# Pooled attention and a gated MLP on one core: the order in which batch 0 of the attention is loaded, cast and normalised

## The chip, the core and the metric

The kernel runs on one core of a Trainium2 chip. A core has a matrix engine (TensorE; PE in the profile, its weight loads PEld), three engines for elementwise work (VectorE: DVE, ScalarE: ACT, GpSimd: POOL), and a queue engine, SyncE (SP), that issues DMAs. PE writes its results into PSUM, from where DVE and ACT read them; all else works on SBUF. Each engine runs its own instructions in program order and waits on semaphores for the others. DMAs are issued from SP's queue or from GpSimd's queue; only the latter convert fp32 to bf16 under way here.

The metric is device time in microseconds (us), the median of several executions. The profile comes from one further execution.

## What is computed

Cut from the reference, with B = 8 batches, H = 8 heads, S = 576 tokens and D = 64:

```python
k_p = k.reshape(B, H, 72, 8, D).mean(axis=3)      # keys and values pooled over 8 tokens
v_p = v.reshape(B, H, 72, 8, D).mean(axis=3)
scores = (1 / sqrt(D)) * q @ k_p.transpose(0, 1, 3, 2)
attn = softmax(scores)                            # over the 72 pooled keys
x = (attn @ v_p).transpose(0, 2, 1, 3).reshape(B * S, H * D)   # 4608 x 512
h = x @ w_in                                      # 512 -> 2048
out = (h * cos(h)) @ w_out                        # 2048 -> 512
```

Inputs and output are fp32; the matmuls take bf16.

## The kernel before

**Tiling.** The 4608 tokens go through the MLP in nine chunks of 512 (`NT`). For each chunk the up projection computes 16 blocks of 128 features in eight pairs (`fp`): `up_mm` makes the 4 matmuls (k chunks 0 to 3 of the 512 inputs) for each block of a pair into one of three two-bank PSUM tiles (`banks[fp % 3]`), `up_g` takes the cosine on ACT (Sin with a bias of pi/2, L363) and multiplies on DVE into `g_sb` (L366), which frees the PSUM tile. The down projection (`down_mm`, L369) follows with 64 matmuls, and `down_out` copies and stores. Attention of batch b+1 is placed between the down matmuls of chunk b, at hand-written positions (`fill`). Engine orders are the program order: the kernel runs under a manual schedule, in which only the semaphores are put in automatically.

**The opening.** Batch 0 has nothing to hide behind. Its work is a chain written out by hand after `warm_up` (L452 on), and the change touches this and the loads ahead of it:

- *Loads.* The first half of k (heads 0 to 3) comes in fp32 over SP's queue into a part of `g_sb` (L401) and is cast by ACT in one piece (L402). GpSimd's queue brings, converted, q's first half, k's second half, q's second half and v (`load_even`, L84), then builds `identity`, then issues the weights (`load_w_in`, L112) and the loads of batch 1.
- *Pooling.* `groups` is a 0/1 matrix made by DVE (L420 to L424). `pool_k_mm` (L159) pools two head pairs by 36 matmuls with the keys as the stationary operand, into 64 rows by 72 columns for each pair. `put_kk` (L132) copies them four times (two halves of rows twice) into `kk`. `pool_v_mm` (L167) pools v; one DVE copy (L169) puts it into `vz`, which a memset had filled with 8.0 (L425).
- *Queries.* `q_transpose_mm` (L202) transposes 18 blocks of 128 columns of q on PE; DVE or ACT copies them into `qT` (L203).
- *Units.* A unit is 256 tokens of four heads: `us[0]` and `us[1]` are the two token ranges of heads 0 to 3, `us[2]` and `us[3]` those of heads 4 to 7 (the last 64 tokens, `REST`, come later). `scores` makes 8 matmuls (L221) and an Exp on ACT (L228) per pair of banks. `sums_first` multiplies the Exp's result by `ones` on PE (L276) and forms the inverse of the sums on ACT as Ln (L280) and Exp (L281). `values_then` makes the values' matmuls (L318) and multiplies by the inverse on DVE into `xT` (L320). `sums_two` and `values_two` (L284 to L309) do both for two units together, over two banks, with one Ln, one Exp and one multiplication of 1024 columns; batch 1 uses them.
- *Warm-ups.* `warm_up(n, bank)` makes n matmuls on constants whose result is not used.
- *Hand-over.* `up_mm(0, 0, 0, 2)` and `up_mm(0, 1, 0, 2)` (L356) start the first two pairs of chunk 0 with k chunks 0 and 1, which need heads 0 to 3 alone; the loop finishes them with k chunks 2 and 3. `exp_tables` and `sin_tables` switch ACT's function table.

Of the kernel before, what the change touches and what calls it, by code (L numbers as in the profile page):

```python
# [9 lines left out]
FP32 = mybir.dt.float32  # L10
BF16 = mybir.dt.bfloat16
# [3 lines left out]
POOL = 8  # L15
# [4 lines left out]
def kernel(  # L20
# [9 lines left out]
    nc = tc.nc  # L30
    B, H, S, D = q.shape
    Sp = S // POOL
# [4 lines left out]
    KCH = d_model // 128  # L37
    FFCH = d_ff // 128
    NT = n_tokens // TILE
    ROW = S // 64  # L40
# [84 lines left out]
    def v_part(b):  # L125
        return vz[b % 2][:, :, 0:4:3, :]
# [25 lines left out]
    def pool_k_mm(b, bank, pj0, pj1):  # L152

        kb = staged["k", b]
        ps = bank[:, 0:(pj1 - pj0) * Sp].rearrange("p (j n) -> p j n", n=Sp)
        for pj in range(pj0, pj1):
            for t in range(ROW):
                for rows in half:
                    nc.tensor.matmul(ps[rows, pj - pj0, :], lhsT=kb[rows, pj, t, :], rhs=groups[rows, t, :],  # L159
                                     start=(t == 0), stop=(t == ROW - 1))  # L160
        return lambda copy: put_kk(b, ps, pj0, pj1, copy)

    def pool_v_mm(b, pair):
        vb = staged["v", b]
        for t in range(ROW):
            for hp, rows in enumerate(half):
                nc.tensor.matmul(pair[:Sp, hp, 0:KCH * D], lhsT=groups[rows, t, :], rhs=vb[rows, :, t, :],  # L167
                                 start=(t == 0), stop=(t == ROW - 1))
        nc.vector.tensor_copy(out=v_part(b).rearrange("p j a d -> p a j d"),  # L169
                              in_=pair[:Sp, :, 0:KCH * D].rearrange("p a (j d) -> p a j d", j=KCH))  # L170
# [25 lines left out]
    def q_transpose_mm(b, bank, g0, g1):  # L196

        if ("qT", b) not in att:
            qT_tile(b)
        ps = bank.bitcast(BF16)[:, 0:(g1 - g0) * 128].rearrange("p (g n) -> p g n", n=128)  # L200
        for g in range(g0, g1):
            nc.tensor.matmul(ps[:, g - g0, :], q_flat(b)[:, g * 128:(g + 1) * 128], identity, is_transpose=True)  # L202
        return lambda copy: copy(out=att["qT", b][:, g0:g1, :], in_=ps)  # L203
# [6 lines left out]
    def scores(b, u, pair):  # L210
        scores_mm(b, u, pair)
        scores_exp(b, u, pair)
# [57 lines left out]
    def sums_first(b, u, cs):  # L270

        (c0, n), (h0, nh) = u
        ex = att["ex", b, u]
        for i in range(nh):
            hp = i % 2
            nc.tensor.matmul(cs[hp * 64:hp * 64 + 64, (i // 2) * n:(i // 2 + 1) * n], lhsT=ones[:Sp, :],  # L276
                             rhs=ex[:, ex_col(u, i):ex_col(u, i) + n])
        w = nh * n // 2
        lnc, inv = inverse_tile(w)
        nc.scalar.activation(out=lnc, in_=cs[:, 0:w], func=ACTF.Ln)  # L280
        nc.scalar.activation(out=inv, in_=lnc, func=ACTF.Exp, scale=-1.0)  # L281
        att["inv", b, u] = inv
# [63 lines left out]
    def sin_tables():  # L346
        nc.scalar.preload_act_table_set("trig_and_small")  # L347
# [49 lines left out]

    kv_even_tiles(0)
    q_tile(0)
    k_first = g_sb.rearrange("p f n -> p (f n)").bitcast(FP32)[:, 0:2 * ROW * D]  # L400
    nc.sync.dma_start(out=k_first.rearrange("p (j n) -> p j n", j=2), in_=even_view(k, 0, 0, 2))  # L401
    nc.scalar.copy(out=staged["k", 0][:, 0:2].rearrange("p j t d -> p (j t d)"), in_=k_first)  # L402

    row_of = consts.tile([128, ROW], FP32, name="row_of")
    for rows in half:
# [2 lines left out]
    first_of = consts.tile([128, Sp], FP32, name="first_of")  # L408
    nc.gpsimd.iota(first_of, pattern=[[POOL, Sp]], base=0, channel_multiplier=0,
                   allow_small_or_imprecise_dtypes=True)  # L410
    load_even(staged["q", 0], 0, q, 0, 2)
    load_even(staged["k", 0], 0, k, 2, 4)
    load_even(staged["q", 0], 0, q, 2, 4)
    load_even(staged["v", 0], 0, v)
    identity = consts.tile([128, 128], BF16, name="identity")
    make_identity(nc, identity)
    dist, sign = (w.rearrange("p f m -> p (f m)").bitcast(FP32)[:, 0:ROW * Sp].rearrange("p (t n) -> p t n", n=Sp)
                  for w in w_out_sb[2:4])
    groups = consts.tile([128, ROW, Sp], BF16, name="groups")
# [2 lines left out]
    nc.vector.scalar_tensor_tensor(out=sign, in0=dist, scalar=1.0 - POOL, in1=dist, op0=ADD,  # L422
                                   op1=mybir.AluOpType.mult)
    nc.vector.tensor_scalar(out=groups, in0=sign, scalar1=0.0, scalar2=None, op0=mybir.AluOpType.is_le)  # L424
    nc.vector.memset(vz[0], float(POOL))  # L425
    ones = consts.tile([128, D], BF16, name="ones")
    nc.vector.memset(ones, float(POOL))
    gate = consts.tile([1, 1], BF16, name="gate")
    half_pi = consts.tile([128, 1], FP32, name="half_pi")
    nc.vector.memset(half_pi, math.pi / 2.0)  # L430

    q_tile(1)
    for cg in range(3):
# [23 lines left out]
    vec, act = nc.vector.tensor_copy, nc.scalar.copy  # L457
    us = BY_HEADS

    warm_up(10, obanks[0])  # L460
    pool_k_mm(0, obanks[1], 0, 2)(vec)
    warm_up(2, banks[1][:, 0, :])
    puts = q_transpose_mm(0, banks[2][:, 0, :], 0, 5), q_transpose_mm(0, obanks[0], 5, 9)
    puts[0](vec)
    puts[1](act)
    warm_up(2, banks[1][:, 0, :])
    scores(0, us[0], banks[0])
    scores(0, us[1], banks[1])
    pool_k_mm(0, obanks[1], 2, 4)(vec)
# [25 lines left out]
    for t in range(NT):  # L495
# [132 lines left out]
```

## Time and profile before

| | |
|---|---|
| Median of 3 runs | 294.7 us (294.66 to 295.22) |
| The profiled execution | 294.47 us; its span from first to last instruction 292.3 us |
| Granted PE clock | 1.000 |
| PE busy in 0 to 20 us | 16.2 us (modelled ends) |
| ACT, DVE, POOL busy in 0 to 20 us | 12.8, 10.7, 14.1 us |
| PE busy in 20 to 40 us | 19.9 us |
| k's first half, SP's queue: issued, cast starts | 0.75, 4.38 us |
| q's first half, GpSimd's queue: issued, first used | 1.41, 7.62 us |
| v, GpSimd's queue: issued, first used | 3.83, 13.32 us |
| First matmul of the up projection | 17.19 us |
| First cosine | 19.98 us |

Times inside the span count from its first instruction. A row of the timeline merges neighbouring instructions of one line and engine: its start, its length, how many, and how long the engine was idle before and until what. The ends of matmuls are modelled, so the row's length on PE can run into the next row; starts are the better guide.

### The profile page before, as it was taken

What the parts mean: (1) busy time and instruction counts of PE and PEld (TensorE: products, weight loads), DVE (VectorE), ACT (ScalarE), POOL (GpSimd) and SP (SyncE); (2) the same over time, 40 slices, a digit from 0 to 9 for tenths busy, and PEclk for the clock granted to TensorE, in tenths of its full rate; (3) what the DMA queues carried; (4) which work ended last, traced back from release to release, by engine and by line L of the source; (5) the groups of instructions that cost most, each with busy time, mean ns of one, the idle gap of its engine ahead of it and who ended that gap; (6) DMA issues with size and microseconds to landing.
All of it is one profiled execution on the core that took longest, in us unless ns stands there. A gap on an engine that the chain in (4) does not pass through costs nothing.

```text
span 292.3 us, 4602 instructions
## 1 busy us (share of the span) xinstructions
PE 282.8 (97%) x1812; PEld 138.1 (47%) x1846; DVE 158.7 (54%) x210; ACT 157.6 (54%) x169; POOL 141.6 (48%) x103
## 2 busy tenths in 40 slices
PE   7889999999999999999999999999999999999995
PEld 2544544445544454445444544454445544444444
DVE  6457675764547544763376437545664557316612
ACT  3786875565546554664467346833675356506500
POOL 8568727997953596369633993299000000000000
PEclk9999999999999999999999999999999999999999
DMA  7999999999766997695659956994705420131032
GB/s 155 206 206 206 204 204 169 175 157 185 119 136 89 183 139 155 89 173 129 141 88 167 163 115 109 171 154 95 140 0 73 93 52 2 36 75 32 2 71 72
DMA packets 57764, 36.05 MB, mean 123 GB/s; under 512 B 35600, under 2 KB 53008, under 8 KB 57744
## 3 DMA queue, kind: packets, MB, share of 16 engines
q0 software_dynamic: 20288, 18.07, 39.7%
q1 hardware_dynamic: 37216, 17.57, 32.3%
q8 instruction: 14, 0.23, 0.3%
q10 hardware_dynamic: 240, 0.13, 0.2%
q14 instruction: 6, 0.05, 0.0%
HBM read 36.70 MB, written 9.44 MB: 158 GB/s over the span
## 4 chain that ended last, share of the span: by engine, by line
PE 93%; DMA 2%; ACT 1%; issue 1%; DVE 1%; POOL 0%; POOLq 0%; DVEq 0%
PE bank L356 42%; PE obank L369 39%; PE bank L221 3%; PE bank L369 2%; PE bank L336 2%; DMA q_b<-in_q_dram 2%; PE bank L387 1%; PE bank L251 1%; ACT ex L228 1%; ACT inv L281 0%; PE bank L290 0%; ACT lnc L280 0%; PE obank L318 0%; PE bank L202 0%; PE bank L304 0%
## 5 line engine op out<-in xcount | busy, mean ns | idle before, releaser
L356 PE MATMUL bank<-xT,w_in_sb 128*128 128x512 bf16 x563 | 125.6, 379 | 0.7
L369 PE MATMUL obank<-w_out_sb,g_sb 128*128 128x512 bf16 x510 | 120.7, 379 | 1.3 <-issue 0.6
L363 ACT ACTIVATE cos<-bank,half_pi 128x1024 f32<-128x1024 f32 x72 | 79.2, 1113 | 68.4 <-PE bank L356 67.8
L366 DVE TENSOR_TENSOR g_sb<-bank,cos 128x1024 bf16<-128x1024 f32 x72 | 87.3, 1223 | 50.3 <-ACT cos L363 50.1
L356 PEld LDWEIGHTS <-w_in_sb 128*128 128x128 bf16 x576 | 56.1, 98 | 68.1 <-issue 1.6
L369 PEld LDWEIGHTS <-g_sb 128*128 128x128 bf16 x560 | 51.3, 98 | 56.7 <-issue 2.0
L141 POOL TENSOR_TENSOR kv_st<-kv_st 72x2048 f32<-72x2048 bf16 (+1 forms) x14 | 52.9, 3779 | 26.5 <-DMA kv_st<-in_k_dram 26.5
L228 ACT ACTIVATE ex<-bank 72x1024 bf16<-72x1024 f32 (+1 forms) x40 | 34.9, 929 | 22.3 <-PE bank L221 22.2
L375 DVE COPY o_sb<-obank 128x512 f32<-128x512 f32 x33 | 22.7, 691 | 44.5 <-PE obank L369 44.3
L144 POOL TENSOR_TENSOR kv_st<-kv_st 72x1024 f32<-72x1024 f32 (+1 forms) x14 | 30.7, 2194 | 1.0
L147 POOL TENSOR_TENSOR kp<-kv_st 72x512 bf16<-72x512 f32 (+1 forms) x16 | 17.8, 1129 | 0.6
L339 DVE TENSOR_TENSOR x_r<-bank,inv_r 128x512 bf16<-128x512 f32 x24 | 16.6, 691 | 0.8
L257 ACT ACTIVATE lnc<-bank 64x256 f32<-64x256 f32 x16 | 6.0, 378 | 19.2 <-PE bank L251 19.1
L344 ACT ACT_TABLE_LOAD x9 | 11.5, 1283 | 0.9 <-PEq L612 0.7
L221 PE MATMUL bank<-qT,kk 64*72 64x256 bf16 (+1 forms) x192 | 11.8, 249 | 0.0
L221 PEld LDWEIGHTS <-kk 64*72 64x72 bf16 x192 | 8.1, 110 | 7.8 <-issue 7.0
L347 ACT ACT_TABLE_LOAD x9 | 11.5, 1283 | 0.2
L336 PEld LDWEIGHTS <-ex 72*128 72x128 bf16 x192 | 8.9, 97 | 5.0
L491 POOL COPY gate<-kk 1x1 bf16<-1x1 bf16 x5 | 0.9, 179 | 20.5 <-DMA kk<-kp 20.5
L337 DVE RECIPROCAL inv_r<-bank 128x8 f32<-128x8 f32 x24 | 4.8, 202 | 10.7 <-PE bank L336 10.7
L262 DVE TENSOR_TENSOR xT<-bank,inv 64x256 bf16<-64x256 f32 x16 | 6.8, 422 | 7.0 <-ACT inv L258 6.9
L104 POOL DMA_DIRECT2D kv_st<-in_v_dram x8 | 6.5, 818 | 7.3 <-DVE vz L150 5.7
(74 smaller groups left out, 129.2 us busy)
## 6 DMA issues: line engine op xcount, KB each, us to landing
out_dram<-o_sb SPq DMA_DIRECT2D x70, 128.0 KB, 2.4
kv_st<-in_v_dram POOLq DMA_DIRECT2D x7, 576.0 KB, 12.7
kv_st<-in_k_dram POOLq DMA_DIRECT2D x6, 576.0 KB, 7.9
q_b<-in_q_dram POOLq DMA_DIRECT2D x6, 576.0 KB, 10.0
w_in_sb<-in_moe_w_in_dram POOLq DMA_DIRECT2D x4, 512.0 KB, 13.4
w_out_sb<-in_moe_w_out_dram POOLq DMA_DIRECT2D x4, 512.0 KB, 14.6
q_b<-in_q_dram POOLq DMA_DIRECT2D x4, 288.0 KB, 12.0
kv_st<-in_k_dram POOLq DMA_DIRECT2D x3, 288.0 KB, 15.5
```

The lines of the kernel that those rows point to most:

```text
L141: add(out=s, in0=x[:, :, 0:4, :], in1=x[:, :, 4:8, :], op=ADD)
L144: add(out=s[:, :, 0:2, :], in0=s[:, :, 0:2, :], in1=s[:, :, 2:4, :], op=ADD)
L147: add(out=kp2[b % 2][:Sp, h0:h1, slot, :], in0=s[:, :, 0, :], in1=s[:, :, 1, :], op=ADD)
L221: nc.tensor.matmul(pair[:Sp, bank, c:c + n].rearrange("p (g n) -> p g n", n=64), lhsT=kk[b % 2][half[r], h0 + i, 0:Sp], rhs=att["qT", b][h ...
L228: nc.scalar.activation(out=ex[:, 0:nh * n].rearrange("p (a n) -> p a n", a=2), in_=pair[:Sp, :, 0:nh * n // 2], func=ACTF.Exp, scale=scale ...
L336: nc.tensor.matmul(out[:, pj, hp * (D + 1):(hp + 1) * (D + 1)], lhsT=ex[:, c:c + 128], rhs=v1)
L339: nc.vector.tensor_mul(out=x, in0=vals, in1=inv.unsqueeze(3).to_broadcast([128, KCH, 2, D]))
L356: nc.tensor.matmul(h[:, j, :], lhsT=w_in_sb[fc // 4][:, ki, (fc % 4) * 128:(fc % 4 + 1) * 128], rhs=xT[:, ki, t * TILE:(t + 1) * TILE], st ...
L363: nc.scalar.activation(out=cos, in_=h, func=ACTF.Sin, bias=half_pi[:, :1])
L366: nc.vector.tensor_mul(out=g_sb[:, 2 * fp:2 * fp + 2, :], in0=h, in1=cos)
L369: nc.tensor.matmul(o, lhsT=g_sb[:, fc, ms * 128:(ms + 1) * 128], rhs=w_out_sb[fc // 4][:, fc % 4, :], start=(fc == 0), stop=(fc == FFCH - 1))
L375: nc.vector.tensor_copy(out=o[:, 0:n], in_=ps)
```

## The change

It touches batch 0 only, up to the third pair of the first up projection.

- q's first half also comes in fp32 over SP's queue, behind k's first half. GpSimd's queue has three loads of batch 0 instead of four, and builds `identity` ahead of them.
- The fp32 pieces are cast in four halves of 576 columns: ACT takes k's first and q's second, DVE k's second and q's first. The memset of `vz[0]` moves between DVE's two casts.
- 8 warm-ups instead of 10 at the start, and 1 instead of 2 before the transposes. The first two head pairs are pooled into two banks and their copies into `kk` go to DVE (pair 0) and ACT (pair 1).
- Units 0 and 1 use `sums_two` and `values_two`. `sums_two` comes after the second half of q's transposes.
- `pool_v_mm` takes two single banks and copies them by two instructions of 256 columns.
- Units 2 and 3 keep `sums_first` and `values_then`, but the first halves of pairs 0, 1 and 2 of the up projection are placed before, between and behind their values; pair 2 is new there, and the loop finishes it with k chunks 2 and 3.

```diff
-    def pool_v_mm(b, pair):
+    def pool_v_mm(b, two):
...
-                nc.tensor.matmul(pair[:Sp, hp, 0:KCH * D], lhsT=groups[rows, t, :], rhs=vb[rows, :, t, :],
+                nc.tensor.matmul(two[hp][:Sp, 0:KCH * D], lhsT=groups[rows, t, :], rhs=vb[rows, :, t, :],
...
-        nc.vector.tensor_copy(out=v_part(b).rearrange("p j a d -> p a j d"),
-                              in_=pair[:Sp, :, 0:KCH * D].rearrange("p a (j d) -> p a j d", j=KCH))
+        for hp in range(2):
+            nc.vector.tensor_copy(out=v_part(b)[:, :, hp, :],
+                                  in_=two[hp][:Sp, 0:KCH * D].rearrange("p (j d) -> p j d", j=KCH))
...
-    k_first = g_sb.rearrange("p f n -> p (f n)").bitcast(FP32)[:, 0:2 * ROW * D]
-    nc.sync.dma_start(out=k_first.rearrange("p (j n) -> p j n", j=2), in_=even_view(k, 0, 0, 2))
-    nc.scalar.copy(out=staged["k", 0][:, 0:2].rearrange("p j t d -> p (j t d)"), in_=k_first)
+    first = g_sb.rearrange("p f n -> p (f n)").bitcast(FP32)[:, 0:4 * ROW * D].rearrange("p (i j n) -> p i j n", i=2, j=2)
+    for i, src in enumerate((k, q)):
+        nc.sync.dma_start(out=first[:, i], in_=even_view(src, 0, 0, 2))
+
+    def cast_first(i, which, j, copy):
+        copy(out=staged[which, 0][:, j].rearrange("p t d -> p (t d)"), in_=first[:, i, j])
...
-    load_even(staged["q", 0], 0, q, 0, 2)
+    identity = consts.tile([128, 128], BF16, name="identity")
+    make_identity(nc, identity)
     load_even(staged["k", 0], 0, k, 2, 4)
     load_even(staged["q", 0], 0, q, 2, 4)
     load_even(staged["v", 0], 0, v)
-    identity = consts.tile([128, 128], BF16, name="identity")
-    make_identity(nc, identity)
...
-    nc.vector.memset(vz[0], float(POOL))
...
+    cast_first(0, "k", 0, act)
+    cast_first(0, "k", 1, vec)
+    nc.vector.memset(vz[0], float(POOL))
+    cast_first(1, "q", 0, vec)
+    cast_first(1, "q", 1, act)
...
-    warm_up(10, obanks[0])
-    pool_k_mm(0, obanks[1], 0, 2)(vec)
-    warm_up(2, banks[1][:, 0, :])
-    puts = q_transpose_mm(0, banks[2][:, 0, :], 0, 5), q_transpose_mm(0, obanks[0], 5, 9)
+    warm_up(8, banks[0][:, 0, :])
+    puts = pool_k_mm(0, obanks[0], 0, 1), pool_k_mm(0, obanks[1], 1, 2)
     puts[0](vec)
     puts[1](act)
-    warm_up(2, banks[1][:, 0, :])
+    warm_up(1, banks[0][:, 0, :])
+    puts = q_transpose_mm(0, banks[2][:, 0, :], 0, 5), q_transpose_mm(0, banks[1][:, 0, :], 5, 9)
+    puts[0](vec)
+    puts[1](act)
+    warm_up(2, banks[0][:, 0, :])
     scores(0, us[0], banks[0])
     scores(0, us[1], banks[1])
-    pool_k_mm(0, obanks[1], 2, 4)(vec)
-    sums_first(0, us[0], banks[0][:, 0, :])
-    for put in (q_transpose_mm(0, banks[2][:, 0, :], 9, 14), q_transpose_mm(0, obanks[0], 14, 18)):
+    pool_k_mm(0, obanks[0], 2, 4)(vec)
+    for put in (q_transpose_mm(0, banks[2][:, 0, :], 9, 14), q_transpose_mm(0, banks[2][:, 1, :], 14, 18)):
         put(vec)
-    sums_first(0, us[1], obanks[1])
-    warm_up(2, banks[1][:, 0, :])
-    scores(0, us[2], banks[0])
+    sums_two(0, tuple(us[0:2]), banks[0])
+    warm_up(2, obanks[1])
+    scores(0, us[2], banks[1])
     scores(0, us[3], banks[2])
-    pool_v_mm(0, banks[1])
+    pool_v_mm(0, obanks)
+    values_two(0, tuple(us[0:2]), banks[0])
     sums_first(0, us[2], obanks[0])
-    values_then(0, us[0], obanks[1])
-    values_then(0, us[1], banks[1][:, 0, :])
-    sums_first(0, us[3], banks[2][:, 0, :])
-    values_then(0, us[2], obanks[1])
-    values_then(0, us[3], obanks[0])
+    sums_first(0, us[3], obanks[1])
     up_mm(0, 0, 0, 2)
+    values_then(0, us[2], obanks[0])
     up_mm(0, 1, 0, 2)
+    values_then(0, us[3], obanks[1])
+    up_mm(0, 2, 0, 2)
     sin_tables()
...
-            up_mm(t, fp, 2 if fp < 2 else 0)
+            up_mm(t, fp, 2 if fp < (3 if t == 0 else 2) else 0)
```

More of the change, by code (lines that the diff above doesn't have):

```diff
@@ L424 @@
     nc.vector.tensor_scalar(out=groups, in0=sign, scalar1=0.0, scalar2=None, op0=mybir.AluOpType.is_le)
-    nc.vector.memset(vz[0], float(POOL))
     ones = consts.tile([128, D], BF16, name="ones")
     nc.vector.memset(ones, float(POOL))
-    gate = consts.tile([1, 1], BF16, name="gate")
     half_pi = consts.tile([128, 1], FP32, name="half_pi")
     nc.vector.memset(half_pi, math.pi / 2.0)
+    gate = consts.tile([1, 1], BF16, name="gate")
+    vec, act = nc.vector.tensor_copy, nc.scalar.copy
+    cast_first(0, "k", 0, act)
[3 more added lines that the diff above has]
+    cast_first(1, "q", 1, act)
     q_tile(1)
@@ L455, in warm_up @@
             nc.tensor.matmul(bank, lhsT=warm[:, 0:128], rhs=warm)
-    vec, act = nc.vector.tensor_copy, nc.scalar.copy
     us = BY_HEADS
-    warm_up(10, obanks[0])
-    pool_k_mm(0, obanks[1], 0, 2)(vec)
-    warm_up(2, banks[1][:, 0, :])
-    puts = q_transpose_mm(0, banks[2][:, 0, :], 0, 5), q_transpose_mm(0, obanks[0], 5, 9)
+    warm_up(8, banks[0][:, 0, :])
+    puts = pool_k_mm(0, obanks[0], 0, 1), pool_k_mm(0, obanks[1], 1, 2)
     puts[0](vec)
     puts[1](act)
-    warm_up(2, banks[1][:, 0, :])
+    warm_up(1, banks[0][:, 0, :])
[3 more added lines that the diff above has]
+    warm_up(2, banks[0][:, 0, :])
     scores(0, us[0], banks[0])
     scores(0, us[1], banks[1])
-    pool_k_mm(0, obanks[1], 2, 4)(vec)
-    sums_first(0, us[0], banks[0][:, 0, :])
-    for put in (q_transpose_mm(0, banks[2][:, 0, :], 9, 14), q_transpose_mm(0, obanks[0], 14, 18)):
+    pool_k_mm(0, obanks[0], 2, 4)(vec)
+    for put in (q_transpose_mm(0, banks[2][:, 0, :], 9, 14), q_transpose_mm(0, banks[2][:, 1, :], 14, 18)):
         put(vec)
-    sums_first(0, us[1], obanks[1])
-    warm_up(2, banks[1][:, 0, :])
-    scores(0, us[2], banks[0])
+    sums_two(0, tuple(us[0:2]), banks[0])
+    warm_up(2, obanks[1])
+    scores(0, us[2], banks[1])
     scores(0, us[3], banks[2])
-    pool_v_mm(0, banks[1])
+    pool_v_mm(0, obanks)
+    values_two(0, tuple(us[0:2]), banks[0])
     sums_first(0, us[2], obanks[0])
-    values_then(0, us[0], obanks[1])
-    values_then(0, us[1], banks[1][:, 0, :])
-    sums_first(0, us[3], banks[2][:, 0, :])
-    values_then(0, us[2], obanks[1])
-    values_then(0, us[3], obanks[0])
+    sums_first(0, us[3], obanks[1])
     up_mm(0, 0, 0, 2)
+    values_then(0, us[2], obanks[0])
     up_mm(0, 1, 0, 2)
+    values_then(0, us[3], obanks[1])
+    up_mm(0, 2, 0, 2)
     sin_tables()
```

## The prediction, made before the changed kernel ran

> **What bounds the kernel now.** I read the engine table and the chain of waits of the whole span first, then the timeline of the first 25 us, because the change touches only that.
>
> ```profile
> span 292.3 us, 4602 instructions
> PE 282.8 (97%) x1812; PEld 138.1 (47%) x1846; DVE 158.7 (54%) x210; ACT 157.6 (54%) x169; POOL 141.6 (48%) x103
> PE 93%; DMA 2%; ACT 1%; issue 1%; DVE 1%; POOL 0%; POOLq 0%; DVEq 0%
> ```
>
> TensorE holds 93% of the chain. The waits of PE after 17.2 us come to one of 0.2 us, so whatever delays PE in the opening delays the end by as much, and the opening is where the other 7% lie. From the timeline of the first 25 us:
>
> ```profile
> 4.38 1.15 ACT L402 CAST kv_st<-g_sb 128x1152 bf16<-128x1152 f32 x1 [2.36 <-DMA g_sb<-in_k_dram]
> 7.62 0.45 PE L202 MATMUL bank<-identity,q_b 128*128 128x128 bf16 x5 [0.68 <-DMA q_b<-in_q_dram]
> 8.33 0.58 ACT L203 COPY qT<-obank 128x512 bf16<-128x512 bf16 x1 [2.80 <-PE obank L202]
> 9.38 1.93 ACT L228 ACTIVATE ex<-bank 72x1024 bf16<-72x1024 f32 x2 [0.46 <-PE bank L221]
> 10.31 1.26 DVE L132 CAST kk<-obank 64x144 bf16<-64x144 f32 x4 [1.71 <-PE obank L159]
> 12.50 0.63 PE L221 MATMUL bank<-qT,kk 64*72 64x256 bf16 x8
> 13.32 1.17 PE L167 MATMUL bank<-kv_st,groups 64*72 64x256 bf16 x18 [0.19 <-DMA kv_st<-in_v_dram]
> 14.59 0.69 DVE L169 CAST vz<-bank 72x512 bf16<-72x512 f32 x1 [2.17 <-ACT inv L281]
> 15.33 0.41 PE L318 MATMUL obank<-ex,vz 72*64 72x256 bf16 x4 [0.22 <-DVE vz L169]
> 16.59 0.63 PE L318 MATMUL obank<-ex,vz 72*64 72x256 bf16 x8 [0.42 <-DVE xT L320]
> 17.19 12.28 PE L356 MATMUL bank<-xT,w_in_sb 128*128 128x512 bf16 x54
> 19.98 2.12 ACT L363 ACTIVATE cos<-bank,half_pi 128x1024 f32<-128x1024 f32 x2 [0.68 <-PE bank L356]
> 21.12 2.35 DVE L366 TENSOR_TENSOR g_sb<-bank,cos 128x1024 bf16<-128x1024 f32 x2 [2.40 <-ACT cos L363]
> 22.40 6.57 PEld L356 LDWEIGHTS <-w_in_sb 128*128 128x128 bf16 x31 [0.15 <-issue]
> ```
>
> Each row is start, duration, engine, line, operation, and in brackets the idle time before it with its releaser. k's first half is cast at 4.38, q's first half is usable at 7.62, the first Exp starts at 9.38. The row to watch is 13.32: v's pooling on PE (call its start P) waited 0.19 us for v's load, and the second pair of scores had ended only at 13.13, so two chains meet there. The row of vz names ACT as its releaser, but PE's pooling ended at 14.49, 0.1 us earlier, and ACT's Ln and Exp had no later use for it: I read P as the cause. PE then runs unbroken from 17.19. At 22.40 comes the first matmul of pair 3 of the up projection. It reuses bank 0, and DVE frees that bank at about 22.3 (21.12 plus 1.22, the page's mean of L366). PE itself was ready at 17.19 + 24 x 0.216 = 22.37 (eight up matmuls take 1.73 in the chain). So the start of pair 3 is set by both within 0.05 us, and from there on a pair costs PE 1.73 against 1.11 on ACT and 1.22 on DVE. The time after is the time before, plus the shift of pair 3's start.
>
> **Tail of the opening, for a given P.** Before: 22.40 - 13.32 = 9.08 us. After, in the new order:
>
> - P to the first vz cast 1.27 (13.32 to 14.59). Two casts of 72x256 instead of one of 72x512: between 0.306 (64x144, L132) and 0.686 (72x512), linear in columns, 0.42 each, 0.84.
> - PE answers 0.05 later. Eight values matmuls to the start of the multiplication: four took 15.33 to 15.85, 0.52, and four more add 0.63 - 0.41 = 0.22; 0.74. The joint multiplication is 128x1024: the same line of batch 1 (L309) took 1.21. Then 0.05 to the first up matmul. Sum so far P + 4.16. Before, the multiplications came singly and the up matmul started at P + 3.87 (17.19).
> - The two sums_first lie before this, under the 1.21 multiplication: cost nothing on PE; without that cover 0.41 each. Ln and Exp for them end some 1.5 us after P + 4.16 at the latest: exps of units 2 and 3 end near 15.3, sums on PE near 16.0, then twice 0.60 + 0.63 on ACT, 18.4; the second multiplication needs it at P + 6.6, 19.3. Covered by 0.9.
> - Half pairs 0, 1 and 2 (k chunks 0 and 1): 12 x 0.216 = 2.59. Between them the two values_then, 4 matmuls each: 0.26 (a further four) to 0.43 (the chain's piece at 15.33); 0.35 each, 0.70. Before, all eight ran at 16.59 while PE waited for DVE, outside this sum.
> - The rest of pair 0, 4 x 0.216 = 0.86: pair 0 is complete at P + 8.31. Before it was complete at 17.19 + 12 x 0.216 = 19.78, P + 6.46, with pair 2 not begun.
> - From pair 0 complete to bank 0 free: 22.40 - 19.78 = 2.62 (cos 1.11, multiplication 1.22, handovers). Before, PE filled this with 4 + 8 matmuls, 2.59. After, 4 of pair 2 are already done, so it has 4 + 4, 1.73: a **stall of 0.89 us at pair 3**. What is late next is pair 4, which needs bank 1: cos and multiplication of pair 1 free it 1.1 after bank 0, PE gets there 1.73 after; no second stall.
>
> Pair 3 starts at P + 10.93 instead of P + 9.08: **+1.85 us for the same P**.
>
> **How much earlier P comes.** Two conditions.
>
> *v's load.* Before GpSimd's stream gets going, the DMA engines have a hole. In the view by stretches, the columns are the stretch, its length, the busy time of PE, PEld, DVE, ACT and POOL (with instructions), the granted clock, the DMA engines' share and GB/s:
>
> ```profile
> 3.00:3.60 0.60, 0.60 (x3) 0.18 (x2) 0.57 (x2) 0.00 (x0) 0.60 (x2) 1.00 1.06 411
> 3.60:4.40 0.80, 0.80 (x3) 0.27 (x2) 0.64 (x2) 0.02 (x1) 0.80 (x2) 1.00 0.77 110
> 4.40:4.90 0.50, 0.50 (x3) 0.20 (x2) 0.44 (x3) 0.50 (x1) 0.42 (x3) 1.00 1.07 157
> 5.00:6.50 1.50, 1.50 (x40) 0.77 (x39) 0.06 (x1) 0.53 (x1) 1.50 (x3) 1.00 1.11 179
> 7.00:13.00 6.00, 4.82 (x80) 3.18 (x83) 3.22 (x10) 4.14 (x6) 3.33 (x5) 1.00 1.22 206
> ```
>
> SP's fp32 transfer runs at 411 GB/s; GpSimd's casting loads count their bf16 bytes, 206, which is 412 of fp32. The bytes up to v are the same after. The hole costs 0.59 us (0.8 us at 110 of 411), the slow rise 0.12 and 0.20: 0.9 in all. q's half on SP's queue is issued at 1.22 and can fill the hole; against that the first GpSimd load is issued 0.55 later, behind the identity (4.59 to 5.14 before), and brings its own slow rise, now beside q's half. Bounds for v: 13.3 (nothing won) and 12.4; I take 12.6, since the hole is the larger part.
>
> The Trainium skill (DMA: Bandwidth & Descriptors, "Issuing engines are not separate DMA queues") says that transfers started by several engines share the same 16 DMA engines, so spreading them saves only issuing time. By that rule alone v would land at 13.3 as before. The rows above agree in the steady stretch, 411 against 2 x 206, but show engines left idle from 3.6 to 4.4, which the rule does not speak of.
>
> *The chain from q.* k's half lands at 4.38 and q's follows on the same queue: 0.59 MB at 411 GB/s is 1.43, 5.8 at best; 6.9 if it shares half and half with GpSimd's loads from 4.0 on; I take 6.1, as GpSimd's stream was slow to rise. ACT and DVE both wait for it before the key copies, since the casts of q stand ahead of them; DVE's memset of vz (0.91) ends near 5.8 and is covered. Then on ACT: cast of 576 columns 0.65 (between 0.585 for 512 and 1.151 for 1152), four key copies of 64x72 at 0.23 (0.59 for 512 and 0.378 for 256 columns, carried on to 72; at most 0.378) 0.92, qT copy 0.585, and 0.47 to the first Exp (8.91 to 9.38): 6.1 + 2.6 = 8.7 against 9.38. From the first Exp to the end of the second scores the DVE chain is unchanged (key copies 10.31, qT, scores to 13.13): 3.75. So 12.45, and 13.25 with q at 6.9. The joint Ln and Exp of units 0 and 1 (1.02 + 1.06 by batch 1's rows instead of 2 x 1.23) start some 0.5 later, as they await the second Exp and PE's sums; inv is wanted near 15.5 and ready near 13.4, so they cost and win nothing. Ten warm-up matmuls become eight: PE idles 4.9 to 5.1, nothing waits.
>
> P is the later of the two, 12.3 to 13.3, **taken 12.7, 0.6 earlier**. Sum: +1.85 - 0.6 = **+1.2 us**. On the profiled execution's 294.47 (span 292.3 and 2.2 around it) that is 295.7; the median shown is 294.7, 0.2 above it, so I write 295.8. A change under 0.2%, 0.6 us, I count as none.
>
> **Rivals.**
>
> - *The loads come so early that they pay the tail* (not slower, 294.5). Place: P. It decides from P = 11.5 for no loss and under 10.9 for a gain above 0.2%. For: all bytes up to v, 3.54 MB at 411 GB/s from 2.5, could be in by 11.1, and 0.4 from last byte to use (k: 3.95 to 4.38) gives 11.5. Against: GpSimd's loads landed about 1.4 us after their share of the bytes had moved (q's half at 7.57, when twice its bytes had gone), and the q chain alone holds P at 12.1. Shorter values or a hidden stall would push the same way. 0.3, of which 0.17 between the bounds and 0.13 faster.
> - *The second SP transfer wins nothing for v* (slower, 296.3). The 16 engines are shared, GpSimd's start is 0.55 later, P stays 13.3: 294.47 + 1.85. For: DMA share 1.1 and more from 4.4 on. Against: the hole. 0.2.
> - *A cold PE* (slower, 296.7). Two warm-ups fewer; before, all ten showed 0.43 each, half speed. If half speed lasted to 8 us, pooling (0.77) and transposes (0.66) double and P is 13.7: +2.2. Against: the pooling at 5.62 already ran at the 0.77 of the later one. 0.05.
>
> My forecast, P from 12.1 to 13.2, has 0.45: 295.1 to 296.3. The range takes in the second rival and most of what lies within 0.2% of the first: 294.2 to 296.8. Slower by over 0.2%: 0.45 + 0.2 + 0.05 = 0.7; within: 0.17; faster: 0.13.
>
> **What would show it.** In the changed profile: k's and q's casts near 4.4 and 6.1; the first Exp near 8.7; PE's L167 near 12.7; the first up matmul near 16.9 and the first cos near 21.1; an idle gap on PE of about 0.9 released by DVE's g_sb before pair 3, which starts near 23.6; after it, no new wait on PE. The prediction is wrong if pair 3 starts before 22.4, if that gap is missing, or if PE waits again later than 25 us.

## The result and the profile after

| | before | after |
|---|---|---|
| Median (lowest to highest), 7 executions each | 294.66 us (294.0 to 295.22) | 296.5 us (295.85 to 302.91) |
| The profiled execution; its span | 294.47; 292.32 us | 295.85; 293.74 us |
| v's pooling on PE starts (P) | 13.32 | 12.52 |
| First matmul of the up projection | 17.19 | 16.51 |
| First cosine | 19.98 | 21.10 |
| First matmul of pair 3 | 22.40 | 23.53 |
| The last chunk's last down step (L387, now L388), by the chain of waits | 285.30 | 286.43 |
| From there to the end of the span | 7.02 | 7.31 |

The change makes the kernel slower: ratio 1.0065, 95% interval 1.0041 to 1.0088. The 302.91 is one disturbed execution (mean granted clock 0.977), which the ratio leaves out.

The page of after, its span and the shares of the chain of waits by engine:

```profile
span 293.7 us, 4600 instructions
PE 93%; DVE 2%; DMA 1%; issue 1%; ACT 1%; DVEq 0%
```

PE holds 93% as before, so the opening is again the first place to look. Its timeline, first the loads and casts (start, duration, engine, line, operation, and in brackets the idle time ahead with its releaser):

```profile
1.64 0.80 POOL masks.py:199 TENSOR_SCALAR_AFFINE_SELECT identity<-identity 128x128 bf16<-128x128 bf16 x1
2.40 0.88 POOL L84 DMA_DIRECT2D kv_st<-in_k_dram  x1
4.89 0.67 ACT L406 CAST kv_st<-g_sb 128x576 bf16<-128x576 f32 x1 [2.87 <-DMA g_sb<-in_k_dram]
6.44 0.67 ACT L406 CAST q_b<-g_sb 128x576 bf16<-128x576 f32 x1 [0.88 <-DMA g_sb<-in_q_dram]
8.98 1.93 ACT L229 ACTIVATE ex<-bank 72x1024 bf16<-72x1024 f32 x2 [0.46 <-PE bank L222]
12.52 1.17 PE L167 MATMUL obank<-kv_st,groups 64*72 64x256 bf16 x18
12.76 0.73 POOL L104 DMA_DIRECT2D kv_st<-in_k_dram  x1 [2.15 <-DMA kv_st<-in_v_dram]
13.70 0.75 DVE L170 CAST vz<-obank 72x256 bf16<-72x256 f32 x2 [1.66 <-PE obank L167]
14.18 0.95 PE L305 MATMUL bank<-ex,vz 72*64 72x256 bf16 x8 [0.48 <-DVE vz L170]
15.24 1.22 DVE L310 TENSOR_TENSOR xT<-bank,inv 128x1024 bf16<-128x1024 f32 x1 [0.79 <-PE bank L305]
16.51 1.02 PE L357 MATMUL bank<-xT,w_in_sb 128*128 128x512 bf16 x4 [0.72 <-DVE xT L310]
17.47 0.41 PE L319 MATMUL obank<-ex,vz 72*64 72x256 bf16 x4
18.78 0.41 PE L319 MATMUL obank<-ex,vz 72*64 72x256 bf16 x4
19.12 3.67 PE L357 MATMUL bank<-xT,w_in_sb 128*128 128x512 bf16 x16
19.30 0.69 DVE L321 TENSOR_TENSOR xT<-obank,inv 128x512 bf16<-128x512 f32 x1 [0.62 <-PE obank L319]
21.10 2.12 ACT L364 ACTIVATE cos<-bank,half_pi 128x1024 f32<-128x1024 f32 x2 [1.87 <-PE bank L357]
23.53 3.83 PE L357 MATMUL bank<-xT,w_in_sb 128*128 128x512 bf16 x17 [0.74 <-DVE g_sb L367]
```

Three things are to be seen. v's pooling starts at 12.52, 0.80 us earlier than before. Its row has no bracket, since the modelled ends of the scores reach past it; but the last piece of v landed at 12.48, 0.04 us ahead of it, as in before (13.28 and 13.32). So v's load sets P here too. GpSimd's row at 12.76, released by v, stands 0.24 behind P; so does its counterpart in before:

```profile
13.56 0.73 POOL L104 DMA_DIRECT2D kv_st<-in_k_dram  x1 [2.06 <-DMA kv_st<-in_v_dram]
```

The first up matmul is earlier too, 16.51 against 17.19. But the first cosine is 1.12 later, and the last row shows a wait that the kernel before did not have: pair 3 stands 0.74 us for DVE, which must free bank 0. So the head start turns into a loss between 16.5 and 23.5. Pair 3 comes 1.13 late, and this is still 1.13 at 286.43, 263 us later: nothing between gives it back. In the chain of waits, before and after (start, duration, what):

```profile
285.30 3.55 PE bank L387 x48
```

```profile
286.43 3.55 PE bank L388 x48
```

The remaining 0.29 of the 1.41 us by which the span grew is added behind that, where the queue engine waits for the last stores. From the waits of SyncE, before and after:

```profile
SPq L623 <- DMA out_dram<-o_sb: 1.2, 1, 1.2
```

```profile
SPq L631 <- DMA out_dram<-o_sb: 1.5, 1, 1.5
```

### The profile page after: what moved, and what is told of

It reads as the page before. It is cut to its first block, busy times and chain, and to the rows that moved or that the text cites. A ratio compares the mean times of both kernels' runs of the same rounds, so it can differ in the third digit from the quotient of the medians.

```text
span 293.7 us, 4600 instructions
## 1 busy us (share of the span) xinstructions
PE 282.7 (96%) x1809; PEld 137.7 (47%) x1843; DVE 159.3 (54%) x212; ACT 158.4 (54%) x172; POOL 141.4 (48%) x102
## 4 chain that ended last, share of the span: by engine, by line
PE 93%; DVE 2%; DMA 1%; issue 1%; ACT 1%; DVEq 0%
PE bank L357 42%; PE obank L370 39%; PE bank L222 4%; PE bank L370 2%; PE bank L337 2%; DMA g_sb<-in_k_dram 1%; PE bank L388 1%; PE bank L252 1%; ACT ex L229 1%; PE bank L305 1%; PE bank L291 1%; DVE g_sb L367 0%; DVE xT L310 0%; ACT cos L364 0%; PE obank L167 0%
## 5 line engine op out<-in xcount | busy, mean ns | idle before, releaser
L345 ACT ACT_TABLE_LOAD x9 | 11.5, 1283 | 0.9 <-PEq L620 0.7
L348 ACT ACT_TABLE_LOAD x9 | 11.5, 1283 | 0.2
## 6 DMA issues: line engine op xcount, KB each, us to landing
kv_st<-in_v_dram POOLq DMA_DIRECT2D x7, 576.0 KB, 12.7
```

## The experiments

Theory: the loads win, the new order of units and half pairs ("the hand-over") loses more. Rivals: the loads lose, or the joint inverses of units 0 and 1 do. X is the first up matmul. The kernel of before was run again beside each group of kernels, and ratios are against those runs. Edits are against after unless another kernel is named.

**1. The opening alone (e1).** The new loads, casts and key pooling, with the units and the hand-over of before:

```diff
-    sums_two(0, tuple(us[0:2]), banks[0])
+    sums_first(0, us[0], banks[0][:, 0, :])
...
-    pool_v_mm(0, obanks)
-    values_two(0, tuple(us[0:2]), banks[0])
+    pool_v_mm(0, banks[1])
...
-            up_mm(t, fp, 2 if fp < (3 if t == 0 else 2) else 0)
+            up_mm(t, fp, 2 if fp < 2 else 0)
```

> The new loads, casts, poolings and transposes, with the old units, v pooling and hand-over of before. Theory (the opening gains, the hand-over loses): v's pooling on PE starts at 12.5 as after, the first up matmul 3.9 later at 16.4; the rest of pair 0 then waits for the last multiplication of unit 3 (first Exp near 9.0 plus 8.6 of ACT work, plus 0.7), so pair 3 starts near 21.8 to 22.0 against 22.40 before and 23.53 after: 0.4 to 0.6 us faster than before, near 294.1. Rival (the loads over SP's queue or the split casts cost the time themselves): pair 3 at 22.4 or later, 295 to 296.

Measured: 294.2 us (median of 10) against 294.31; ratio 1.0017 (0.9971 to 1.0062), wide because two executions took 298.5. Its timeline:

```profile
12.70 1.17 PE L167 MATMUL bank<-kv_st,groups 64*72 64x256 bf16 x18 [0.29 <-DMA kv_st<-in_v_dram]
16.57 10.77 PE L356 MATMUL bank<-xT,w_in_sb 128*128 128x512 bf16 x48
21.78 5.28 PEld L356 LDWEIGHTS <-w_in_sb 128*128 128x128 bf16 x25 [0.15 <-issue]
```

P is 0.62 earlier than before and pair 3, at 21.78, also 0.62: P + 9.08, exactly the distance of before. The up matmuls run on without a gap. So the loads win what they were forecast to win, and the whole loss of pair 3 belongs to the hand-over; this is read from the trace, as the interval of the times includes 1. Yet the span, 292.0, is only 0.3 shorter: this kernel too has the longer end (7.31).

**2. The tail alone (e2).** The mirror of e1: before, with the new hand-over and v's two single banks alone.

```diff
-    pool_v_mm(0, banks[1])
+    pool_v_mm(0, obanks)
+    values_two(0, tuple(us[0:2]), banks[0])
...
     up_mm(0, 0, 0, 2)
+    values_then(0, us[2], obanks[0])
     up_mm(0, 1, 0, 2)
+    values_then(0, us[3], obanks[1])
+    up_mm(0, 2, 0, 2)
```

> The old loads, casts and pooling of k, with the joint step of units 0 and 1, the two copies of v and the interleaved hand-over of the change. Theory: v's pooling starts at 13.3 as before and pair 3 comes 10.9 to 11.0 later, 24.2 to 24.3, with a wait of 0.7 to 0.9 for g_sb ahead of it: 1.8 us slower than before, 296.3 to 296.6. Rival (the hand-over costs nothing and the opening is at fault): pair 3 at 22.6 or earlier, 294.7.

Measured: 297.51 us (296.61 to 297.85, four executions), ratio 1.0103 (1.008 to 1.0125). The one execution at full clock, 296.61, is at the edge of what was expected; the other three stand at a mean clock of 0.994. The profiled one is of these. In the view by stretches (stretch, length, busy time of PE, PEld, DVE, ACT and POOL, granted clock, DMA share, GB/s):

```profile
16.00:17.00 1.00, 0.29 (x4) 0.11 (x2) 0.96 (x1) 0.97 (x2) 1.00 (x2) 1.00 1.22 203
17.00:18.00 1.00, 0.98 (x4) 0.34 (x3) 0.00 (x0) 0.94 (x3) 1.00 (x2) 0.67 1.26 209
18.00:19.00 1.00, 1.00 (x6) 0.18 (x4) 0.00 (x0) 0.98 (x2) 1.00 (x2) 0.50 1.23 203
19.00:20.00 1.00, 0.67 (x4) 0.35 (x4) 0.69 (x1) 0.74 (x1) 1.00 (x2) 0.50 1.27 202
20.00:21.00 1.00, 1.00 (x6) 0.21 (x5) 0.00 (x0) 0.00 (x0) 0.10 (x1) 0.62 1.25 207
```

The clock column falls to half just when the up projection begins: 0.67 and 0.62 at the edges put the stretch from about 17.3 to 20.8, some 3.4 us. It cost 1.6: pair 3 came at P + 12.60 (25.62) where after has P + 11.01. That is a second price of the hand-over, paid in some executions, which the prediction had not counted: it leaves PE thin before the up projection (2.18 us busy of the 3.41 ahead of 17.34).

**3. No early half of pair 2 (e3).** The forecast said that the early half takes away PE's work under the first multiplication into `g_sb` and so makes the 0.74 stall. If so, leaving it out removes the stall, but the time is the same, as PE then waits earlier.

```diff
-    up_mm(0, 2, 0, 2)
...
-            up_mm(t, fp, 2 if fp < (3 if t == 0 else 2) else 0)
+            up_mm(t, fp, 2 if fp < 2 else 0)
```

> The changed kernel without the early half of pair 2. Theory (pair 0's second half is set by unit 3's multiplication, and the early half of pair 2 only fills that time): the wait for g_sb ahead of pair 3 vanishes, a wait of about 0.8 for unit 3's xT appears ahead of pair 0's second half, and pair 3 still starts at 23.4 to 23.6; the time is that of after within 0.2. Rival (the stall at pair 3 is a cost of its own, brought by the half pair): pair 3 at 22.7 to 22.8, 0.7 to 0.8 us faster than after.

Measured: 296.49 us (295.87 to 297.97, four executions), against 296.5 for after. In the waits of PE the one on `g_sb` is gone, and one of the same size has come ahead of it:

```profile
PE bank L357 <- DVE xT L321: 0.9, 1, 0.9
```

The stall is thus a symptom: the work of PE was moved, and the last multiplication into `xT` bounds both orders. In after, too, pair 0's second half starts at 20.04, at once behind that multiplication (19.30, 0.69 long). (Its profiled execution had the half clock too, so the trace shows the place and not the size.)

**4. All values ahead of the up projection (e4).** Units 2 and 3 take banks 1 and 2, and the order of before returns, with the joint step kept:

```diff
+    values_then(0, us[2], banks[1][:, 0, :])
+    values_then(0, us[3], banks[2][:, 0, :])
     up_mm(0, 0, 0, 2)
-    values_then(0, us[2], obanks[0])
     up_mm(0, 1, 0, 2)
-    values_then(0, us[3], obanks[1])
-    up_mm(0, 2, 0, 2)
```

> The changed kernel with the values of units 2 and 3 put ahead of all up matmuls, into two banks that are free by then, and no early half of pair 2. Theory (values behind the half pairs are what makes pair 0 late): PE makes them under the joint multiplication, unit 3's multiplication is then set by ACT's inverse (17.93 in after) and ends near 18.6, pair 0 is complete near 19.6, the first cosine comes near 19.75 against 21.10, pair 3 near 22.2: 1.2 to 1.4 us faster than after, 0.1 to 0.3 faster than before. Rival (the joint inverse and multiplication of units 0 and 1 set the time): pair 3 within 0.3 of 23.5.

Measured: 294.79 us (294.65 to 295.08, ten executions), ratio 1.002 (1.001 to 1.0029).

```profile
15.54 0.71 PE L319 MATMUL bank<-ex,vz 72*64 72x256 bf16 x8
20.02 2.12 ACT L364 ACTIVATE cos<-bank,half_pi 128x1024 f32<-128x1024 f32 x2 [0.54 <-PE bank L357]
22.45 4.63 PEld L357 LDWEIGHTS <-w_in_sb 128*128 128x128 bf16 x22 [0.15 <-issue]
```

The values run at 15.54, where PE waits anyway for the joint multiplication. Pair 3 starts at P + 9.68 (P is 12.77) instead of P + 11.01: of the 1.93 that the tail costs, 1.33 come from the place of the values and of the half pairs. The other 0.60 stands ahead of pair 0's second half (P + 6.19 against P + 5.60), which waits for unit 3's multiplication, and that for ACT's inverse. ACT's first Ln for units 2 and 3 begins at P + 2.86 instead of P + 2.14: PE makes its sums behind the joint values, and in before ahead of the values. Sums ahead of the joint values were not tried.

**5. Single inverses (e5).** Is the joint step of units 0 and 1 the loss? The order of after, but each unit with its own sums, Ln, Exp and multiplication, in the two halves of bank tile 0:

```diff
-    sums_two(0, tuple(us[0:2]), banks[0])
+    sums_first(0, us[0], banks[0][:, 0, :])
+    sums_first(0, us[1], banks[0][:, 1, :])
...
-    values_two(0, tuple(us[0:2]), banks[0])
+    values_then(0, us[0], banks[0][:, 0, :])
+    values_then(0, us[1], banks[0][:, 1, :])
```

> The changed kernel with single sums, inverses, values and multiplications for units 0 and 1 in the same banks and places, all else as changed. Theory (most of the tail's cost is the place of units 2 and 3's values, little is the joint step): the first up matmul comes 3.9 to 4.0 after v's pooling as with the joint step, pair 3 still starts 10.9 to 11.1 after it, near 23.4, and undisturbed executions take 295.7 to 296.2. Rival (the joint step is what costs): pair 3 starts 10 or less after v's pooling and the time falls by 0.8 or more, to 295.1 or less.

Measured: 296.45 us (296.36 to 298.99, four executions), ratio 1.0087 (1.0056 to 1.0118). X came at P + 4.51, a miss: 3.9 to 4.0 had been expected.

```profile
16.00 0.41 PE L319 MATMUL bank<-ex,vz 72*64 72x256 bf16 x4 [0.85 <-DVE xT L321]
24.28 2.97 PE L357 MATMUL bank<-xT,w_in_sb 128*128 128x512 bf16 x13 [0.73 <-DVE g_sb L367]
```

The first row gives the reason: the second unit's values waited 0.85 for the first unit's multiplication, although they write the other half of the tile. In this arrangement single inverses are 0.5 worse than the joint step (P + 11.52 against 11.01), and the stall stays. This does not clear the joint step, as the wait of 0.85 is e5's own; e4 does so for most of the loss, since it keeps the joint step and has X at P + 3.99, 0.12 later than before. What single inverses in separate tiles would do within this order was not tried.

**6. Keeping PE busy (e7 and e10).** Five more warm-up matmuls, whose results are not used, in after (e7) and in e2 (e10):

```diff
     pool_v_mm(0, obanks)
+    warm_up(2, banks[0][:, 0, :])
...
     sums_first(0, us[3], obanks[1])
+    warm_up(3, banks[1][:, 0, :])
```

> The changed kernel with two warm-up matmuls between v's pooling and the joint values, and three behind the sums of unit 3, where PE idled 0.5 and 0.7. Theory (in some executions PE's idle time before the first up matmul lets the clock fall to half from about 17 to 20.5, which costs 1 to 2 us): with PE kept busy the granted clock stays at 0.997 or more in every execution that is not otherwise disturbed, none is at 0.994, pair 3 is near 23.5, the median 295.9 to 296.2 with a spread of about 0.5. Rival (the clock falls whatever PE does there): executions at 0.994 and 297 or more remain as often as after, about 1 in 4.

> The run of the hand-over alone (old loads), with two warm-up matmuls between v's pooling and the joint values and three behind the sums of unit 3. Theory (PE's idle time ahead of the first up matmul lets the clock fall to half in that kernel, 3 of 4 executions at 0.994): with PE busy there no execution is at 0.994, the traced one shows full clock from 16 to 22 and pair 3 near 24.2, and the median falls from 297.5 to 296.4 to 296.7. Rival (the fall of the clock has another cause): most executions stay at 0.994 and near 297.5.

Measured: e7 296.11 us (295.8 to 300.32, five executions), ratio 1.0051 (1.0038 to 1.0064), pair 3 at P + 11.01 as in after; e10 296.3 us (296.17 to 300.21, six executions), ratio 1.0048 (1.0032 to 1.0064), where e2 had 1.0103. No execution of the eleven shows the clock of 0.994, against three of four in e2 (which ran on another chip than e10). So the half clock makes up the excess of e2, and it is not what makes after slower: with it gone e7 still loses half a per cent. One execution of each, 300.32 in e7 and 300.21 in e10, stands at 0.989. The second is the one that was profiled, and shows another cause; its row of v's pooling and its stretches:

```profile
14.88 1.47 PE L167 MATMUL obank<-kv_st,groups 64*72 64x256 bf16 x18 [1.98 <-DMA kv_st<-in_v_dram]
```

```profile
14.00:16.00 2.00, 1.12 (x18) 1.01 (x17) 0.00 (x0) 1.57 (x2) 0.73 (x1) 0.91 1.26 207
16.00:18.00 2.00, 2.00 (x14) 0.79 (x12) 0.75 (x2) 0.00 (x0) 0.98 (x2) 0.50 1.24 205
18.00:20.00 2.00, 2.00 (x15) 0.95 (x12) 1.23 (x1) 1.19 (x2) 2.00 (x3) 0.50 1.25 202
20.00:22.00 2.00, 1.78 (x5) 0.53 (x4) 0.00 (x0) 1.92 (x4) 1.17 (x2) 0.50 1.24 205
```

v landed at 14.84, where the four other traces with the old loads have 12.94 to 13.54; PE waited 1.98 us for it, and the clock was then at half for some 6.8 us. Why v was late stays open.

**7. Identity behind the loads (e8).** In after the first GpSimd load is issued at 2.40 instead of 1.41. e8 is e1 with the identity behind the loads again:

```diff
-    make_identity(nc, identity)
     load_even(staged["k", 0], 0, k, 2, 4)
     load_even(staged["q", 0], 0, q, 2, 4)
     load_even(staged["v", 0], 0, v)
+    make_identity(nc, identity)
```

> The new opening with the old hand-over (as in the run of the opening alone), with identity built behind GpSimd's three loads, whose first is then issued at 1.41 instead of 2.40. Theory (v's landing is set by the bytes ahead of it, and q's half over SP's queue keeps the engines busy already): v's pooling starts within 0.3 of the opening alone (12.7), time within 0.3 of its 294.2. Rival (GpSimd's late start holds v back): v's pooling starts at 12.2 or earlier, pair 3 near 21.4, 293.8 or less. A third way: GpSimd's loads take half of the engines from q's half, q's casts start at 6.8 or later instead of 6.0 and the first Exp at 9.2 or later.

Measured: 294.13 us (293.92 to 294.67, 12 executions) against 294.39; ratio 0.999 (0.9981 to 0.9998). P 12.50, pair 3 21.59. P is 0.2 earlier than in e1, but the six traces with the identity ahead (after, e1, e3, e4, e5, e7) scatter from 12.52 to 13.06, so no effect of GpSimd's load issued 1.0 earlier is shown. v's landing (12.46) still sets P.

**8. Before, again (e9).** For the scatter of the marks.

> The kernel before, once more, for a second trace of it and for the scatter between two copies of one kernel. Theory: pair 3 starts within 0.4 of 22.40 and the last chunk's matmuls 262.9 after it; v's pooling at 13.0 to 13.4; time equal to before within 0.1%. Rival (the scatter between executions is as large as the effects here): pair 3 off by 0.6 or more.

Measured: 294.37 us, ratio 0.9995 (0.9983 to 1.0006); P 13.29, pair 3 22.38, last down step 285.28, all within 0.03 of the first trace.

**9. A better version (e11).** e8 with v's copy cut into two pieces by heads, so that units of heads 0 to 3 start after the first:

```diff
-        nc.vector.tensor_copy(out=v_part(b).rearrange("p j a d -> p a j d"),
-                              in_=pair[:Sp, :, 0:KCH * D].rearrange("p a (j d) -> p a j d", j=KCH))
+        for j in range(0, KCH, 2):
+            nc.vector.tensor_copy(out=v_part(b)[:, j:j + 2].rearrange("p j a d -> p a j d"),
+                                  in_=pair[:Sp, :, j * D:(j + 2) * D].rearrange("p a (j d) -> p a j d", j=2))
```

> The opening with identity behind the loads and the old hand-over, in which v's copy into vz is cut in two by heads (pairs 0 and 1, then 2 and 3) instead of one of 512 columns. Theory (the chain from v's pooling to the first up matmul is on the path): values of unit 0 start 0.27 earlier, the second copy lies under them, the first up matmul comes 3.6 after v's pooling instead of 3.9; from there ACT's inverse of unit 3 allows some 0.05 to 0.25 of gain in pair 3, near 21.4 against 21.59, time 0.0 to 0.2 us under the 294.1 of that run. Rival (ACT's chain already sets pair 3): pair 3 not earlier, and a wait on unit 3's xT of 0.25 ahead of pair 0's second half.

Measured: 293.54 us (293.49 to 293.62, five executions) against 294.79 on that chip; ratio 0.9956 (0.9943 to 0.997).

```profile
14.03 0.75 DVE L170 CAST vz<-bank 72x256 bf16<-72x256 f32 x2 [2.48 <-ACT ex L229]
14.50 0.41 PE L319 MATMUL obank<-ex,vz 72*64 72x256 bf16 x4 [0.23 <-DVE vz L170]
16.36 10.98 PE L357 MATMUL bank<-xT,w_in_sb 128*128 128x512 bf16 x49
```

X is at P + 3.60 (P 12.76) instead of P + 3.87, and pair 3 at P + 8.82 instead of P + 9.09; as P came 0.26 later than in e8's trace, pair 3 itself is at 21.58, as there. The time beats both kernels, and by more than the traces explain: 1.25 us by the medians, 0.53 by the spans (291.80 against 292.32). Some 0.3 of it lies outside the span, which an execution of e11 exceeds by 1.8 us and one of before by 2.1; why stays open.

**10. The longer end (e12, e13).** In the program as built, SyncE's DMAs, and the last three stores, which go from ACT's queue, take turns among eight completion semaphores. One more load in the opening moves the turn of the last store by one. e12 is before with one 256-byte load whose data nobody reads (shown); e13 is e11 with seven such loads.

```diff
+    spare = consts.tile([1, 1, 64], FP32, name="spare")
+    for i in range(1):
+        nc.sync.dma_start(out=spare[:, i], in_=k[0, 0, i:i + 1])
```

> The kernel before with one more load on SP's queue behind k's, 256 bytes into a tile that nobody reads. In the traces so far the span ends 7.0 to 7.1 us after the last chunk's first matmul where SP's queue has one load in the opening, and 7.3 to 7.4 where it has two. Theory (the count of DMAs on the hardware queues decides, through the turn of the eight completion semaphores): 7.3 here, span 0.25 to 0.3 longer, 294.7 to 295.0 beside a before of 294.4. Rival (the new opening delays the stores in another way): 7.0 to 7.1 and the time of before.

> The kernel with v's copy cut by heads (293.54 beside a before of 294.79), with seven more such small loads on SP's queue, so that the semaphores' turn at the end is that of before. Theory: the span ends 7.0 to 7.1 after the last chunk's first matmul instead of 7.32, 0.25 to 0.3 us faster, if the small loads leave the opening alone. Rival: 7.3 as without them.

Measured: e12 294.63 us (12 executions) against 294.35, ratio 1.0007 (0.9997 to 1.0017); from the last down step to the end 7.32 instead of 7.02. e13 293.16 us (293.05 to 293.28, six executions) against 294.35, ratio 0.9954 (0.994 to 0.9967); 7.05. The waits of SyncE for the last stores, e12 and then e13:

```profile
SPq L626 <- DMA out_dram<-o_sb: 1.5, 1, 1.5
```

```profile
SPq L635 <- DMA out_dram<-o_sb: 1.2, 1, 1.2
```

One tiny load lengthens the end by 0.3, seven more take it away again: the number of DMAs decides, not what they carry (SyncE issues 110 in before, 111 in after and e12, 118 in e13). In the traces this is clear; in the times it is at the edge, since 0.3 us is 0.1% (e12's interval includes 1, and e13's ratio is e11's within the intervals). Why one turn is dearer can be read from the traces: at the end SyncE waits for the eight semaphores one after the other, some 0.06 apart. In before the first of them stands for SyncE's last store, which landed 1.77 after its issue, and the last of them for ACT's; in after the first stands for ACT's last store, which landed 2.05 after its issue, and the seven other waits follow that.

## Why the prediction came out right

- **"The start of pair 3 is set by both" and nothing later gives it back.** Right. From pair 3 to the last down step before took 262.90 us, after 262.90, and the twelve other traces from 262.89 to 262.91. Two readings were off without harm: PE has five waits of 0.2 after 17.2 and not one, the same five after; and not all of the other 7% lies in the opening, as the last 7 us are an end that can change too.
- **The tail, P + 10.93.** Measured P + 11.01, against 9.08 before: +1.93 where +1.85 was forecast. In parts: X at P + 3.99 (4.16), pair 0 complete about X + 4.39 (4.15), pair 3 2.62 behind that (2.62). The first came sooner because the first copy began at P + 1.18 instead of 1.27 and the two took 0.75 instead of 0.84. The second came later because each values group between the half pairs cost more than its 0.35: the two and the half pairs up to 19.12 took 2.61 where 2.43 was summed. The last 0.05 is the wait for the multiplication of 19.30.
- **The stall of 0.89.** There, 0.74 long by the waits, which count from a modelled end, and 0.90 by the starts of the matmuls (22.63 to 23.53), released by `g_sb` as forecast; e3 shows that it can be moved and not saved within this order.
- **P at 12.7, "the later of the two".** It is 12.52 in after's trace and 12.50 to 13.06 in e1, e3, e4, e5, e7, e8, e11 and e13, 12.73 on average; with the old loads 13.02 to 13.58 (before, e2, e9, e12; e10's 14.88 left out), 13.30 on average. So the gain is about 0.57, with 0.6 forecast, and the 0.80 of after's own trace is the lucky end of the scatter. The later of the two is v: P follows v's last landing by 0.04 in all of these but e2 and e5, where the scores end some hundredths later. v landed at 12.46 to 13.02 with the new loads (12.6 had been taken). The chain from q came out shorter than summed, because v's pooling can start 0.03 to 0.11 behind the start of the last scores matmul (e2, e5) and not at its modelled end. The hole did fill, in the stretches of after:

```profile
3.60:4.40 0.80, 0.80 (x3) 0.28 (x2) 0.18 (x3) 0.00 (x0) 0.80 (x2) 1.00 0.86 317
4.40:4.90 0.50, 0.50 (x2) 0.00 (x0) 0.01 (x1) 0.01 (x1) 0.50 (x2) 1.00 1.02 396
```

  317 and 396 GB/s stand where 110 and 157 stood; at 411 GB/s the difference is worth 0.7 us, an estimate near the 0.57 measured. (The engines were not idle in the hole: their share was 0.77, at 110 GB/s.) The Trainium skill (DMA: Bandwidth & Descriptors, "Issuing engines are not separate DMA queues"), by which only issuing time would be saved, holds for the steady stretch and not for this hole: e1 has pair 3 0.62 earlier.
- **k's cast near 4.4, q's near 6.1, first Exp near 8.7.** Each late in after's trace (4.89, 6.44, 8.98); the eight other traces with the new loads have 4.45 to 4.61, 5.88 to 6.03 and 8.43 to 8.73. So the steps were sized well, and k's cast, at 4.25 to 4.38 with the old loads, is some 0.2 later with q's transfer behind it. One term was mis-sized: GpSimd's first load came 1.0 later (2.40 against 1.41) and not 0.55, as the select that builds `identity` took 0.80 instead of 0.29.
- **The sum, +1.2.** In the profile it is +1.41: -0.80 for P, +1.93 for the tail, and +0.29 at the end of the kernel (rounded). The last term was missing from the prediction, whose "time before, plus the shift of pair 3's start" left no room for it. The medians lie 1.84 apart, half as much again as forecast, and 296.5 lies above the forecast's own 295.1 to 296.3, in the part of the range that had been added for the second rival. That the number is inside the range is thus partly luck; the mechanism is what the traces bear out. The profiled execution is the shortest of after's seven. One of the longer ones (297.72) has the mean clock of 0.994 that e2's traced execution has; why 296.5 (at 1.000) and 297.07 (at 0.998) are longer is not explained.
- **The rivals.** *The loads pay the tail* needed P at 11.5; no kernel came below 12.50. *The second transfer wins nothing* needed P to stay at 13.3; e1 refutes it by 0.62. *A cold PE* was feared in the pooling of k, at 5.6: those 36 matmuls took 0.83 (0.77 before). The half clock did come, in e2 and e3, but twelve microseconds later, in the gap before the up projection, a place at which the prediction did not look.

## What to carry to other kernels

An opening that feeds a bound engine is worth what the first unbroken matmul stream wins, so cost every step to the point from which the engine never waits again; here, to pair 3. Work slipped between the first matmuls of that stream is paid in full, the same work under a wait just ahead of it is free, and a half started early is no gain when it only empties the cover of the next wait. Test the parts of a combined change apart: the loads here were good (e8), the hand-over was bad, and together they were a loss.

## What the hardware did that was not expected

- The clock can fall in the middle of a kernel: half clock from about 17.3 to 20.8 us in e2, though PE had been busy 2.18 of the 3.41 us before. The Trainium skill (TensorE: Matmul & The Clock Gate, "What's actually happening") speaks of a free-running window of about 3.4 us and of the half clock after an idle window; the length agrees, but PE was not idle for a window here. In each of the fourteen traces the record of the clock begins at a mark of its own, between 4.36 and 7.10 us, and its stretches are whole multiples of 3.41 us. Cut along these marks, the opening has half clock behind the windows in which PE was busy 1.44, 1.95 and 2.18 us (e10, e3, e2; modelled ends), and the full clock went on behind all others, of which the thinnest has 2.32 (e4). Why e10 stayed at half for a second window, with PE busy throughout the first, is open. So it also matters where the marks fall, which the kernel does not choose. In e5 PE was thinner than in e2, but the thin stretch (the second row) lies across two windows (the first and the third):

```profile
12.20:15.61 3.41, 2.41 (x31) 1.59 (x31) 1.10 (x3) 2.91 (x4) 0.73 (x1) 1.00 1.24 207
13.90:17.31 3.41, 1.60 (x19) 0.96 (x18) 2.13 (x4) 1.83 (x3) 1.23 (x2) 1.00 1.24 206
15.61:19.03 3.42, 2.61 (x23) 1.33 (x23) 1.32 (x3) 2.22 (x4) 2.95 (x4) 1.00 1.24 207
```

  This is read from traces and was not tested, and busy time is not the whole measure: near the kernel's end, full clock followed a window with 1.64 (e13).
- The end of the kernel depends on how many DMAs SyncE has issued since its start: 7.0 or 7.3 us behind the same matmul. The last store from ACT's queue lands some 0.3 us later behind its issue than the last one from SyncE's, and the turn of the semaphores decides whether that is covered.
- GpSimd's affine select took 0.80 us in after (and in e1 and e4) and 0.29 in e8, where it runs beside no DVE work with two inputs. In after DVE's product of two fp32 inputs (L423) ran from 1.46 to 2.29, and the select, begun at 1.64, ended at 2.44. This agrees with the Trainium skill (SBUF — State Buffer, "Who interferes with whom"): a DVE instruction with two inputs from SBUF contends with a GpSimd instruction that reads SBUF.
- Two halves of one two-bank tile are not independent in the program as built, where the semaphores are put in automatically: in e5 PE waited 0.85 for a reader of the other half. Whether the chip itself would need that wait, no run here shows.
